# A fused attention and GeGLU block on one core: Tanh behind a row's first mark, x's transfers in front at block changes, softmax numerators divided inside the attention, output weights in the key tiles

## The chip, the core and the metric

The kernel runs on one core of a Trainium2 chip. The core has five engines with instruction streams of their own: PE (TensorE, matrix products; PEld is its loading of the stationary operand), DVE (VectorE), ACT (ScalarE), POOL (GpSimd) and SP (SyncE, which here issues all DMA transfers, in one queue). They wait for one another by semaphores. The metric is device microseconds of one execution, lower is better, given as the median of several.

## The reference

The input is x of 2048 tokens with 576 features. It is normalized (layer norm without parameters), and two things are computed from it: multi-head attention s with 32 heads of 18 features, and a gated feed-forward g with 4608 hidden values. The output is x + s * silu(g).

```python
def _A_ref(x, wqkv, wo):
    qkv = (lambda x, *d: x.transpose(*d))((x @ wqkv).reshape(B, S, 3, H, Dh), 2, 0, 3, 1, 4)
    q, k, v = qkv[0], qkv[1], qkv[2]
    scores = jnp.einsum("bhqd,bhkd->bhqk", q, k) * (Dh ** -0.5)
    p = _softmax(scores, axis=-1)
    o = jnp.einsum("bhqk,bhkd->bhqd", p, v)
    return (lambda x, *d: x.transpose(*d))(o, 0, 2, 1, 3).reshape(B, S, D) @ wo

def _B_ref(x, w_gate, w_up, w_down):
    return (_gelu(x @ w_gate) * (x @ w_up)) @ w_down

x = A_x
xn = _layernorm(x, axis=-1)
s = _A_ref(xn, A_wqkv, A_wo)
g = _silu(_B_ref(xn, B_w_gate, B_w_up, B_w_down))
return x + s * g
```

## The kernel before

**Precision.** Products are made in a 32-bit format that keeps fewer digits, so each operand is split into a high and a low part (`split` L101 on POOL, `split_av` L111 on ACT and DVE), and three products (high x high, low x high, high x low) are summed.

**Stages.** First (to about 196 us) x is normalized and transposed, q, k and v are projected and written to DRAM. Then come 144 *sections*. A section (`section` L500, products in `gate_up` L385) makes the gate and up products of 128 hidden values for one block of 512 tokens: 27 pairs of 64-row products, two of which run side by side in the upper and lower half of the array. Two sections are a *row* (256 hidden values); 18 rows make a token block, and there are 4 blocks. Sections 0 to 9 lead in; 10 to 137 (`ATT`) carry the attention; 138 to 143 carry the output projection.

**Attention.** 32 units (4 query blocks x 8 groups of 4 heads), four sections each. In a section 16 score products and 16 products for the maxima of a later unit are dealt out between the gate and up pairs. ACT turns scores into exponentials (L659), DVE reduces maxima (L624). After each odd section PE multiplies exponentials by values (L693, 64 products). Column 0 of the values is 1, so that row 0 of the result is the softmax's denominator; the numerators go to `oT` in DRAM, the denominators to `sT`, and their reciprocals (L727) to `rT`. `max_neg` and `max_end` (L626, L634) turn a unit's maxima into two more rows of its queries, by PE, ACT (`mr`) and eight transfers. Keys lie in seven buffers of two tiles each (`KS`, L564), loaded twelve transfers at a time (`load_k` L575).

**Hidden values.** `activate` (L405), behind each section: ACT squares the gate (L408); DVE makes the inner polynomial (L409); ACT copies up (L412); DVE multiplies it by the gate (L413); ACT takes Tanh (L414); DVE makes the product (L416). `finish` (L535) splits the result into hh and hl on POOL.

**Sums of a row.** In the attention a row's sums (`half_downs` L447) follow the next even section. The 8 sums (4 groups of 128 tokens x 2 column halves) are each made in two halves, of 64 rows of the contraction, six products each; halves of two sums run side by side. The second half of a sum may start only when its first is in. This is told by a *mark*: a tiny ACT instruction (L443) that waits for the last product of the first half, and for which the second half's first product waits. DVE adds each sum to Y (L427).

**x of a block.** `load_xd` (L132) loads the transposed x of the next block, six tiles, into the lower half of the partitions and copies each to the upper half on POOL (L139). There is one set of tiles: it is reloaded behind section 35, 71 and 107.

**The end.** `load_wo` (L795) loads the output weights, `load_o` (L804) a block of numerators with, row group by row group, the reciprocals broadcast over 18 rows each (`den`, L820, 13 transfers), and DVE multiplies (L822). A *place* is 128 tokens: `split_o` (L824) on POOL, `load_xy` (L830) loads x and y and makes the gate th, `project_o` (L842) makes two halves of 14 products on PE, `put` (L849) multiplies by the gate on DVE, adds x and stores. The loop at L870 does three places a section, and the last four behind the last section.

**Order.** The order of PE's instructions is that of the program (manual schedule). For all other engines a planner of the framework orders each engine's instructions by estimated times. Three means bind it: `keep_in_program_order`, `after` (L94, a wait by semaphore), and a dependency without a semaphore, which only fixes the order on one engine.

Of the kernel before, what the change touches and what calls it, by code (L numbers as in the profile page):

```python
# [8 lines left out]
F32 = mybir.dt.float32  # L9
# [8 lines left out]
P = 128  # L18
# [25 lines left out]
MROW = 3 * DH  # L44
NK = KT + 1
# [22 lines left out]
def kernel(ctx: ExitStack, tc: tile.TileContext, x, wqkv, wo, w_gate, w_up, w_down, out):  # L68
# [14 lines left out]
    rT = dram.tile([H, S], F32, name="rT")  # L83
    ys = dram.tile([S - TB, D], F32, name="ys")
# [3 lines left out]
    ident = const.tile([P, P], F32, name="ident")  # L88
    make_identity(nc, ident)
    identr = const.tile([P, P], F32R, name="identr")  # L90
    nc.gpsimd.tensor_copy(identr, ident)
# [5 lines left out]


    low_part = []
# [32 lines left out]
    def load_xd(b):  # L132

        xd = [[], []]
        for c in range(0, NC, XG):
            for i in range(2):
                t = wts.tile([P, XG, TB], F32R, name=f"xd{i}_{c}")
                nc.sync.dma_start(f(t)[0:HR], xhs[b][i, c * HR:(c + XG) * HR, :].rearrange("(k p) t -> p k t", p=HR))
                nc.gpsimd.tensor_copy(t[HR:P], t[0:HR])  # L139
                xd[i].append(t)  # L140
        return xd
# [8 lines left out]
    with tc.tile_pool(name="pro", bufs=1) as pro, tc.tile_pool(name="pps", bufs=1, space=PSUM) as pps:  # L150

# [186 lines left out]
        for b in range(NB):  # L338
# [25 lines left out]
            if b == 1:  # L364
                XD = load_xd(0)
            if b == 2:
# [11 lines left out]

    FF = {"w": ahead, "xd": XD, "down": [], "n": 0,
# [25 lines left out]
    def activate(pg, pu, early):  # L405
# [8 lines left out]
        nc.scalar.activation(t1, t1, AF.Tanh, scale=GC * GS)  # L414
        if early:
            nc.vector.scalar_tensor_tensor(t1, t1, 1.0, t2, op0=ALU.add, op1=ALU.mult)  # L416
        else:
            nc.vector.scalar_tensor_tensor(t1, t1, 1.0, pg, op0=ALU.add, op1=ALU.mult)
            nc.vector.tensor_tensor(t1, t1, pu, op=ALU.mult)
        return t1  # L420
# [26 lines left out]
    def half_downs(b, r, hs, wd, Y, middle=None):  # L447
# [52 lines left out]
    def section(specials=(), tag="f", raw_d=None, early=None):  # L500
# [8 lines left out]
        keep = tc.keep_in_program_order if n == NU * NA + len(FIRST) + 1 else lambda i: i  # L509
        nxt = load_gu((n + 1) % (NR * G), keep) if n + 1 < NF else None  # L510
        if nxt:
            for k in range(NG - 1):
                first = split_gu(nxt, k)
                if k == 0 and n in ATT and n > ATT.start:
                    tc.add_manual_dep(first.ins, FF["hl"].ins.name, mybir.DependencyInfo(
                        mybir.DependencyClass.NoSync, mybir.DependencyReason.DATA), reason="hidden values first")
# [18 lines left out]
    def finish(pool=ffn, cut=split, bufs=1):  # L535
# [5 lines left out]
        cut(hh, hl, FF["act"])  # L541
# [10 lines left out]

    todo = {}
# [8 lines left out]

    with tc.tile_pool(name="att", bufs=1, reuse_waits="tile") as att:
        KS = [[att.tile([P, TB], F32R, name=f"KS{i}{r}") for r in range(2)] for i in range(KB)]  # L564
# [4 lines left out]
        M2 = [att.tile([P, 2, HR], F32R, name=f"m2{i}") for i in range(2)]  # L569
        for mm in M2:  # L570
            nc.vector.memset(f(mm), 0.0)
# [25 lines left out]
        for i in range(TB // HR):  # L597
            nc.sync.dma_start(zq[:, i * HR:(i + 1) * HR], ident[0:HR - MROW, HR:P])

        QS, MX, ACC, SUM, PT, NM, DEN = {}, {}, {}, {}, {}, {}, {}  # L600
# [25 lines left out]
        def max_neg(u, keep=lambda i: i):  # L626
# [3 lines left out]
            m2 = NM[u] = M2[u % 2]  # L630
# [3 lines left out]
        def max_end(u, tags="mf"):  # L634

            m2 = NM.pop(u).rearrange("p i c -> p (i c)")
            pms = [ps.tile([P, TB], F32, name="pm", tag=tag, bufs=BANKS[tag])[:, 0:HR] for tag in tags]
            for a, pm in enumerate(pms):
                rr = slice(HR * a, HR * a + HR)
                nc.tensor.matmul(pm, m2[rr], identr[rr, rr], start=True, stop=True)  # L640
            mr = att.tile([P, P], F32, name="mr", bufs=1)
            for a, pm in enumerate(pms):
                nc.scalar.activation(mr[:, HR * a:HR * a + HR], pm, AF.Copy)
# [285 lines left out]
```

## Time and profile before

| what | us |
|---|---|
| median of 3 runs (2714.59 to 2718.29) | 2714.97 |
| the profiled execution | 2709.72 |
| its span, first to last instruction | 2707.9 |
| PE busy | 2573.5 |
| DVE busy | 1952.4 |
| ACT busy | 1567.7 |
| POOL busy | 1289.0 |

The span is what the profile's rows are placed in; 1.8 us of the execution lie around it. Busy times overlap, as the engines work side by side. A row of the timeline gives the start from the span's begin, the length, the engine, the line of the kernel, the operation, what is written <- read, and in brackets how long the engine stood idle and what ended that. A row of the waits gives the instruction that waited, who released it, the total, the number and the longest. PE issues a product before the last one has left the array, so a row's length is longer than its share of time; starts of neighbours give the pace.

### The profile page before, as it was taken

How to read it: one execution, taken by the hardware profiler on the slowest of the kernel's cores; microseconds unless marked ns; L12 is line 12 of the kernel's file. 1: busy time of each engine (PE TensorE's matmuls, PEld its weight loads, DVE VectorE, ACT ScalarE, POOL GpSimd, SP SyncE). 2: the span in 40 equal slices, each digit the busy share in tenths (PEclk: the TensorE clock that was granted, in tenths of full speed). 3: DMA queues.
4: the chain of work that ended last, by engine and by line, in shares of the span. 5: the costliest groups of instructions: out<-in, count | busy, mean ns of one | idle time of the engine just before them, and what ended most of it. 6: DMA issues, size and time to landing. Idle time of an engine off the chain costs nothing.

```text
span 2707.9 us, 63064 instructions
## 1 busy us (share of the span) xinstructions
PE 2573.5 (95%) x24038; PEld 2014.9 (74%) x24038; DVE 1952.4 (72%) x3470; ACT 1567.7 (58%) x3114; POOL 1289.0 (48%) x1404
## 2 busy tenths in 40 slices
PE   9999999999999999999999999999999999999578
PEld 8888777777777777777767777777777777777468
DVE  5327877788877777787877777888777777882345
ACT  3223566666656666666656666666656666666111
POOL 2127454444454444444464444444454444445354
PEclk9999999999999999999999999999999999999889
DMA  8766344344454444444464434444454444433553
GB/s 268 255 233 149 87 108 100 98 100 97 100 128 100 100 100 100 100 97 99 98 135 100 98 98 99 96 98 100 97 120 113 100 100 99 100 79 66 156 178 113
DMA packets 379564, 315.53 MB, mean 117 GB/s; under 512 B 107388, under 2 KB 289148, under 8 KB 379264
## 3 DMA queue, kind: packets, MB, share of 16 engines
q1 hardware_dynamic: 379264, 311.51, 45.6%
q8 instruction: 191, 3.13, 0.5%
q14 instruction: 109, 0.89, 0.1%
HBM read 261.38 MB, written 49.47 MB: 115 GB/s over the span
## 4 chain that ended last, share of the span: by engine, by line
PE 70%; DVE 20%; DMA 3%; issue 2%; ACT 2%; POOL 2%; SPq 1%; ACTq 0%; POOLq 0%; DVEq 0%
DVE mx L624 18%; PE pg L395 17%; PE acc L693 16%; PE py L438 14%; PE po L171 7%; PE pe L658 6%; PE pm L623 5%; PE pu L395 3%; DVE t L409 1%; PE po L846 1%; DMA den<-rT 1%; ACT t L408 1%; DMA xd<-xhs 1%; ACT pT L659 1%; DMA yy<-ys 1%
## 5 line engine op out<-in xcount | busy, mean ns | idle before, releaser
L659 ACT ACTIVATE pT<-pe 128x512 f32<-128x512 f32 x2048 | 1151.5, 598 | 389.2 <-PE pm L623 271.7
L624 DVE TENSOR_REDUCE mx<-pm 128x1 f32<-128x512 f32 x2048 | 1251.4, 682 | 168.9 <-PE pm L623 166.3
L395 PE MATMUL pu<-xd,wh 64*128 64x512 f32 x2592 | 932.6, 392 | 13.0 <-POOL xd L139 13.0
L395 PE MATMUL pg<-xd,wh 64*128 64x512 f32 x2592 | 931.5, 391 | 0.9 <-DVE thl L853 0.9
L623 PE MATMUL pm<-KS,q 64*128 64x512 f32 x2048 | 784.1, 388 | 0.0
L658 PE MATMUL pe<-q,KS 64*128 64x512 f32 x2048 | 779.3, 388 | 0.0
L395 PEld LDWEIGHTS pg<-xd,wh 64*128 64x128 f32 x2592 | 477.8, 185 | 118.2 <-POOL wh L102 49.6
L102 POOL TENSOR_SCALAR hh<-t 128x512 fp32r<-128x512 f32 x128 | 79.5, 621 | 925.4 <-DVE t L416 911.3
L395 PE MATMUL pu<-xd,wl 64*128 64x512 f32 x1296 | 503.0, 388 | 0.0
L395 PE MATMUL pg<-xd,wl 64*128 64x512 f32 x1296 | 502.7, 388 | 0.0
L395 PEld LDWEIGHTS pu<-xd,wh 64*128 64x128 f32 x2592 | 478.2, 185 | 20.3 <-POOL xd L139 15.7
L693 PE MATMUL acc<-pT,VS 128*32 128x512 f32 x4096 | 452.8, 594 | 0.0
L104 POOL TENSOR_TENSOR wl<-raw,wh 128x384 fp32r<-128x384 f32 x432 | 434.4, 1020 | 13.2
L438 PE MATMUL py<-dh,hh 64*128 64x288 f32 (+1 forms) x2160 | 351.0, 299 | 65.0 <-ACT mark L443 62.8
L623 PEld LDWEIGHTS pm<-KS,q 64*128 64x128 f32 x2048 | 375.6, 185 | 31.4 <-DVE mx L624 4.0
L658 PEld LDWEIGHTS pe<-q,KS 64*128 64x128 f32 x2048 | 371.5, 185 | 23.6
L438 PE MATMUL py<-dh,hl 64*128 64x288 f32 (+1 forms) x2160 | 344.3, 294 | 0.0
L693 PEld LDWEIGHTS acc<-pT,VS 128*32 128x32 f32 x4096 | 127.3, 110 | 289.9 <-issue 276.2
L438 PE MATMUL py<-dl,hh 64*128 64x288 f32 (+1 forms) x2160 | 342.3, 292 | 0.0
L427 DVE TENSOR_TENSOR Y<-py,Y 128x288 f32<-128x288 f32 x544 | 235.2, 455 | 136.5 <-PE py L438 136.4
L102 POOL TENSOR_SCALAR wh<-raw 128x384 fp32r<-128x384 f32 x432 | 218.1, 517 | 219.3 <-PE pu L395 156.4
L438 PEld LDWEIGHTS py<-dh,hh 64*128 64x128 f32 (+1 forms) x2160 | 219.3, 185 | 88.2 <-ACT mark L443 77.3
(121 smaller groups left out, 3115.2 us busy)
## 6 DMA issues: line engine op xcount, KB each, us to landing
KS<-qk SPq DMA_DIRECT2D x1536, 36.0 KB
raw<-in_B_w_gate_dram SPq DMA_DIRECT2D x144, 288.0 KB
raw<-in_B_w_up_dram SPq DMA_DIRECT2D x144, 288.0 KB
raw<-in_B_w_down_dram SPq DMA_DIRECT2D x67, 576.0 KB
VS<-vs SPq DMA_DIRECT2D x128, 152.0 KB
qk<-t SPq DMA_DIRECT2D x72, 256.0 KB
q<-qk SPq DMA_DIRECT2D x384, 36.0 KB
xx<-in_A_x_dram SPq DMA_DIRECT2D x32, 288.0 KB
```

The costliest lines, as they stand in the source:

```text
L102: first = nc.gpsimd.tensor_scalar(hi, raw, 1.0, 1.0, op0=ALU.mult, op1=ALU.mult)
L104: low_part[:] = [keep(nc.gpsimd.tensor_tensor(lo, raw, f(hi), op=ALU.subtract))]
L171: nc.tensor.matmul(o, st, m, start=(i == 0), stop=(i == len(terms) - 1))
L395: nc.tensor.matmul(o, w[1 + wp][k][rr, c, :], xd[xp][k][rr, c, :], start=(i == 0), stop=(i == len(terms) - 1))
L408: nc.scalar.activation(t1, pg, AF.Square)
L427: nc.vector.tensor_tensor(yy, py, yy, op=ALU.add)
L438: return nc.tensor.matmul(py, hs[g][a][rr, j * P:(j + 1) * P], wd[w][rr, g, 288 * c:288 * c + 288], start=start, stop=stop)
L623: nc.tensor.matmul(pm, QS[u, r][rr, t * P:(t + 1) * P], KS[(u * NA + c) % KB][r][rr, :], start=True, stop=True)
L624: nc.vector.tensor_reduce(MX[u][:, 2 * r + a, t, c:c + 1], pm, axis=AX.X, op=ALU.max)
L658: nc.tensor.matmul(pe, KS[(u * NA + c) % KB][r][rr, t * P:(t + 1) * P], QS[u, r][rr, :], start=True, stop=True)
L659: nc.scalar.activation(PT[u, kt][:, 2 * r + a, :], pe, AF.Exp, scale=SCALE)
L693: nc.tensor.matmul(ACC[u][32 * a:32 * a + 32, :], VS[(u * NA + c) % VB][:, v:v + 32], pt[:, a, :], start=first, stop=last, skip_group_chec ...
```

## The change

Five edits.

1. `activate` returns Tanh and what follows as a function, `rest`. Where a row's sums by halves come next, `rest` is called inside them, behind the first mark, with Tanh bound behind that mark on ACT. Elsewhere it is called at once.
2. Before the section at whose end x is exchanged, the keys are loaded first; the six transfers of x are bound behind them, the next gate and up weights behind the last of x, and the split of hh behind the last copy.
3. In the attention the numerators of units 0 to 29 are read back, in two pieces of 72 rows x 256 tokens, with their reciprocals broadcast, multiplied on POOL and stored to `oN`. Those of the last two units follow in the first section of the end, on DVE. `load_o` reads `oN`, in two transfers.
4. The output weights are loaded into the key tiles as these come free in the last six attention sections and behind them, by 16 transfers. The key tiles get a pool of their own, one tile for both halves.
5. In the end a row's sums come before the places; the places use another group of three accumulator banks; `put` adds on DVE; the two column halves are stored by one transfer, but for the last block; split numerators get three buffers instead of two, gates three instead of four.

Besides, m2 has one buffer with 48 columns a half, `mr` shares two buffers with the pieces, and the identity lives in the first stage only, with two copies of its 64x64 corner kept.

```diff
     def load_xd(b, key=None):
...
-                nc.sync.dma_start(f(t)[0:HR], xhs[b][i, c * HR:(c + XG) * HR, :].rearrange("(k p) t -> p k t", p=HR))
-                nc.gpsimd.tensor_copy(t[HR:P], t[0:HR])
+                asked[:] = [nc.sync.dma_start(f(t)[0:HR], xhs[b][i, c * HR:(c + XG) * HR, :]
+                                              .rearrange("(k p) t -> p k t", p=HR))]
+                if key:
+                    no_sync(asked[0], key, "keys first")
+                copied[:] = [nc.gpsimd.tensor_copy(t[HR:P], t[0:HR])]
...
-        nc.scalar.activation(t1, t1, AF.Tanh, scale=GC * GS)
-        if early:
-            nc.vector.scalar_tensor_tensor(t1, t1, 1.0, t2, op0=ALU.add, op1=ALU.mult)
...
+        def rest(behind=None):
+            tanh = nc.scalar.activation(t1, t1, AF.Tanh, scale=GC * GS)
+            if behind:
+                no_sync(tanh, behind, "a mark first")
+            if early:
+                nc.vector.scalar_tensor_tensor(t1, t1, 1.0, t2, op0=ALU.add, op1=ALU.mult)
...
                             elif a == 1:
                                 seen[k] = behind(one)
+                                if k == 0 and "rest" in FF:
+                                    FF.pop("rest")(seen[k])
...
+        if asked:
+            xd_last = asked.pop()
+
+            def keep(i):
+                no_sync(i, xd_last, "transposed x first")
         nxt = load_gu((n + 1) % (NR * G), keep) if n + 1 < NF else None
...
-            FF["xd"] = load_xd(b + 1)
-        FF["act"] = activate(pg, pu, n < ATT.stop)
+            FF["xd"] = load_xd(b + 1, FF["key"])
+        FF["act"], FF["rest"] = activate(pg, pu, n < ATT.stop)
+        if n not in ATT or g or not FF["down"] or not FF["down"][0][-2]:
+            FF.pop("rest")()
...
-        cut(hh, hl, FF["act"])
+        first = cut(hh, hl, FF["act"])
+        if n in ATT and copied:
+            no_sync(first, copied.pop(), "transposed x first")
...
+    def load_numbers(num, rb, g, toks):
+
+        nc.sync.dma_start(num, oT[QD * DH * g:QD * DH * (g + 1), toks])
+        nc.sync.dma_start(rb, rT[QD * g:QD * (g + 1), toks].rearrange("h (o s) -> h o s", o=1)
+                          .to_broadcast([QD, DH, toks.stop - toks.start]))
+
+    def norm_numbers(num, rb, g, toks, engine):
+        engine.tensor_tensor(num, num, rb, op=ALU.mult)
+        nc.sync.dma_start(oN[QD * DH * g:QD * DH * (g + 1), toks], num)
...
+    KT2 = [key.tile([P, 2, TB], F32R, name=f"KS{i}") for i in range(KB)]
+    KS = [[t[:, r] for r in range(2)] for t in KT2]
...
+                    for h in range(2 if u < NU - 2 else 0):
+                        at((u + 1) * NA + 3 + h, 2 * h, load_piece, u, h)
+                        at((u + 1) * NA + 4 + h, 2 * h, norm_piece, u, h)
...
+            new_x = (FF["n"] + 1) % (NR * G) == 0
+            if new_x:
+                load_k(n - 1 + KB, behind_it)
             section([p for s in range(s0, s0 + SLOTS) for p in slot_pairs(s)])
-            if n > 0:
+            if n > 0 and not new_x:
                 load_k(n - 1 + KB)
+            if n > NU * NA - KB:
+                load_wo((n - 1) % KB)
...
         def load_o(b):
...
-            nc.sync.dma_start(o[:, 0:KT, :], oT[0:R0, toks].rearrange("(k p) t -> p k t", p=P))
-            nc.sync.dma_start(o[0:HR, KT, :], oT[R0:D, toks])
-            for k in range(NK):
...
-                    nc.sync.dma_start(den[rows], rT[h:h + m, toks].rearrange("h (o s) -> h o s", o=1)
-                                      .to_broadcast([m, e - d, TB]))
-                nc.vector.tensor_tensor(o[0:n, k, :], o[0:n, k, :], den[0:n], op=ALU.mult)
+            nc.sync.dma_start(OT[b % 2][:, 0:KT, :], oN[0:R0, toks].rearrange("(k p) t -> p k t", p=P))
+            nc.sync.dma_start(OT[b % 2][0:HR, KT, :], oN[R0:D, toks])
...
             if n == NU * NA:
-                load_wo()
+                load_wo((n - 1) % KB)
...
                 load_o(0)
                 ready(2)
-            elif n < ENDS - 1:
+                for u in range(NU - 2, NU):
+                    piece = [S2[0:QD * DH, i, 0:TB] for i in range(2)]
+                    where = u % NQ, slice(S - TB, S)
+                    load_numbers(*piece, *where)
+                    norm_numbers(*piece, *where, nc.vector)
+            downs()
+            if NU * NA < n < ENDS - 1:
                 for b, j in places[done:done + 3]:
                     for c in range(2):
-                        put(b, j, c, project_o(b, j, c, "mf"[n % 2]), nc.gpsimd)
+                        put(b, j, c, project_o(b, j, c, "s"), nc.vector)
                     done += 1
                     ready(done + 2)
-            downs()
             finish(epi, cut, 2)
```

More of the change, by code (lines that the diff above doesn't have):

```diff
@@ L130, in split_gu, with load_xd @@
         return first
-    def load_xd(b):
+    def load_xd(b, key=None):
         xd = [[], []]
@@ L365 @@
                 XD = load_xd(0)
+                for i in range(TB // HR):
+                    nc.sync.dma_start(zq[:, i * HR:(i + 1) * HR], ident[0:HR - MROW, HR:P])
             if b == 2:
@@ L736, with behind_it @@
             load_q(0, (r,))
+        def behind_it(one):
+            FF["key"] = one
         slot, chunk = 0, 1
```

107 lines of the change are left out of this document (58 added, 49 removed).

## The prediction

> **What bounds the kernel now.** I read the first line of the page, then the busy time of each engine by stage, then what TensorE (PE) waited for.
>
> ```profile
> span 2707.9 us, 63064 instructions
> ```
>
> The table by stage has: stretch, length, busy time (instructions) of PE, PEld, DVE, ACT and POOL, granted clock, DMA share, GB/s. The rows are the attention from its second section on (127 sections) and the last six sections with the output projection.
>
> ```profile
> 312.97:2516.35 2203.38, 2127.60 (x21075) 1624.36 (x21073) 1698.66 (x2999) 1444.98 (x2885) 1078.44 (x1167) 1.00 0.42 100
> 2516.35:2707.90 191.55, 134.95 (x968) 123.60 (x964) 84.36 (x141) 27.09 (x45) 88.58 (x102) 0.87 0.53 155
> ```
>
> PE is the bound in the attention. It idles 2203.38 - 2127.60 = 75.8 us in the attention, and 191.55 - 134.95 = 56.6 us in the last stage, where its clock is down too (0.87). Its waits, by window (attention, then the end): total us, times, longest.
>
> ```profile
> PE py L438 <- ACT mark L443: 62.8, 63, 1.2
> PE pu L395 <- POOL xd L139: 13.0, 5, 3.8
> ```
> ```profile
> PE po L846 <- DVE thl L853: 25.9, 5, 10.3
> PE po L846 <- POOL oh L102: 21.0, 1, 21.0
> ```
>
> So three places can be won: one mark a row (63 rows), three block changes, and the end. The change has a part for each.
>
> **Part 1, Tanh behind the first mark.** One row's place, from the timeline: start, length, engine, line.
>
> ```profile
> 1427.07 0.61 ACT L412 ACTIVATE t<-pu 128x512 f32<-128x512 f32 x1
> ...
> 1427.22 0.69 DVE L409 SCALAR_TENSOR_TENSOR t<-t,pg 128x512 f32<-128x512 f32 x1 [0.29 <-ACT t L408]
> ...
> 1427.41 0.29 PE L438 MATMUL py<-dl,hh 64*128 64x288 f32 x2
> ...
> 1427.54 0.29 PE L438 MATMUL py<-dh,hl 64*128 64x288 f32 x2
> ...
> 1427.94 0.63 ACT L414 ACTIVATE t<-t 128x512 f32<-128x512 f32 x1 [0.27 <-DVE t L409]
> 1428.48 0.42 ACT L443 ACTIVATE mark<-mark 128x1 f32<-128x1 f32 x2
> 1428.61 0.69 DVE L416 SCALAR_TENSOR_TENSOR t<-t,t 128x512 f32<-128x512 f32 x1
> ...
> 1428.71 0.40 PE L438 MATMUL py<-dh,hh 64*128 64x288 f32 x2 [0.89 <-ACT mark L443]
> ...
> 1429.81 0.46 DVE L425 COPY Y<-py 128x288 f32<-128x288 f32 x1 [0.51 <-PE py L438]
> ```
>
> PE issues a pair of products each 0.13 us (1427.41 to 1427.54), so it wanted to go on at 1427.67 and did at 1428.71: 1.04 us lost. Marks 0 and 1 stand behind Tanh, and Tanh waits for the DVE product L409, which ends at 1427.91. With mark 0 in front of Tanh, it starts where the copy L412 ends, some 0.1 us early as rows on ACT do (Tanh's end 1428.57, mark's start 1428.48): 1427.58, done 0.21 later, PE at about 1427.80. Residue 0.13. The **next late thing** is mark 1: Tanh still starts at 1427.94, so mark 1 ends at 1428.69 as now, while PE wants it 6 x 0.13 after 1427.80, at 1428.58: 0.1 at most, less if PE's first pair after a stop is slow, as now (1428.71 to the next pair). I take 0.85 us a row. Behind the waiting Tanh stand the later marks on ACT, L416 on DVE and the split of hh on POOL; L416 moves by nothing, since L409 sets Tanh's start, and DVE idles 0.51 before the first sum Y. Sum: 63 x 0.85 = **53.5 us**; between 38 (0.6 a row, if mark 1 takes over more) and 65 (1.04). The score work does not swallow it: in such an even section DVE is busy 14.56 and ACT 12.63 of 17.81 us (first row of the next part).
>
> **Part 2, block changes.** The even section in front of which x is exchanged, thrice, and an ordinary one of the same kind first:
>
> ```profile
> 1305.93:1323.74 17.81, 16.63 (x186) 14.44 (x184) 14.56 (x27) 12.63 (x28) 6.83 (x10) 1.00 0.24 69
> 1374.90:1399.09 24.19, 19.04 (x186) 15.72 (x184) 15.04 (x27) 12.76 (x28) 16.17 (x18) 0.93 0.62 144
> 747.27:772.03 24.76, 19.06 (x186) 15.66 (x184) 14.95 (x27) 12.76 (x28) 16.16 (x18) 0.93 0.60 142
> 2002.10:2026.33 24.23, 20.11 (x186) 16.47 (x184) 15.04 (x27) 12.76 (x28) 16.15 (x18) 0.86 0.61 143
> ```
> ```profile
> 1381.39 1.47 POOL L139 CAST xd<-xd 64x1536 fp32r<-64x1536 f32 x1
> ...
> 1386.21 1.46 POOL L139 CAST xd<-xd 64x1536 fp32r<-64x1536 f32 x1
> ...
> 1387.72 0.50 PE L395 MATMUL pu<-xd,wh 64*128 64x512 f32 x1 [3.56 <-POOL xd L139]
> ```
>
> The three lose 6.4 + 6.9 + 6.4 = 19.7 us. The last copy (1386.21) starts 3.4 us behind the end of the copy before it, with other splits of POOL between. In the new order the six copies (8.8 us) run in front of hh. The x transfers pass the weight transfers on SP and stay behind twelve key transfers, now issued a section earlier. Moved back are hh, hl and the next weights, which are needed a section later: covered, and if that cover failed they would cost what PE waits now. PE works 7.08 us on values between the sections,
>
> ```profile
> 1409.20 7.08 PE L693 MATMUL acc<-pT,VS 128*32 128x512 f32 x64
> ```
>
> and wants the last third of x two thirds into the next. I leave 0.6 us each: **18 us**; between 10 (the transfers themselves late) and 20.
>
> After that stop the granted clock is 0.53 for the next 3.41 us:
>
> ```profile
> 1388.29:1391.70 3.41, 3.41 (x20) 2.71 (x18) 2.21 (x4) 1.79 (x3) 1.95 (x3) 0.53 0.14 13
> ```
>
> The Trainium skill, TensorE: Matmul & The Clock Gate, Part 1 (The HAM clock gate), says that an idle window of about 3.4 us halves the clock until a busy one has passed. The trace agrees here (3.56 us idle, 3.41 us slow).
>
> **Part 3, the end.** By section (the granted clock is the third number from the right):
>
> ```profile
> 2516.35:2526.07 9.72, 9.72 (x81) 8.12 (x78) 6.35 (x7) 1.23 (x2) 4.32 (x6) 1.00 0.41 114
> 2526.07:2581.96 55.89, 25.23 (x165) 22.81 (x163) 18.12 (x27) 4.48 (x7) 22.01 (x25) 0.73 0.74 211
> 2581.96:2613.94 31.98, 24.55 (x161) 22.92 (x162) 16.61 (x27) 4.86 (x7) 15.95 (x16) 0.84 0.45 134
> 2613.94:2648.99 35.05, 22.75 (x164) 20.74 (x163) 12.03 (x22) 3.00 (x5) 22.97 (x28) 0.85 0.60 184
> 2648.99:2673.06 24.07, 21.41 (x164) 19.52 (x163) 11.14 (x18) 6.45 (x9) 15.59 (x21) 1.00 0.52 154
> 2673.06:2707.90 34.84, 31.29 (x241) 29.48 (x239) 20.12 (x44) 7.07 (x15) 7.73 (x9) 1.00 0.22 66
> ```
>
> From the chain of waits, and from SP's waits:
>
> ```profile
> 2528.48 10.88 DMA den<-rT
> ...
> 2679.75 3.38 PE py L438 x24
> 2683.13 7.43 PE po L846 x56
> ```
> ```profile
> SPq L855 <- POOL thl L854: 45.2, 17, 10.2
> ```
>
> Removed: 52 denominator transfers and 20 DVE products, the first of which stood between the last attention work and the first projection (the 10.88 us); five transfers of output weights there (16 smaller ones now fall into the last six attention sections and the first behind them). Added there: six transfers and two DVE products for the last two units, needed only by the fourth block. The 24 additions go from POOL to DVE, so stores wait for DVE, where SP had stood 45.2 us on POOL with the next x, y and weights behind it; whole rows save 12 stores.
>
> What PE needs at full clock: a section is at most 2679.75 - 2673.06 = 6.7, half a row's sums 3.4, three places 6 x 14 products by 7.43/56 = 11.1; together 21.2. The first and last rows of the table stay. 9.7 + 4 x 21.2 + 34.8 = 129.3. The fourth such section already takes 24.07, 2.9 over it, with POOL's additions in it. I leave 10 us of idle time: 139.3, a gain of **52 us**; between 24 (only the start mended: 55.89 to 31.98) and 62. New first in line is the transfer of the first numerators, then POOL's splits; both lie beside section and sums.
>
> The additions' price on DVE has these rows (shortest, median, longest):
>
> ```profile
> L854 POOL TENSOR_TENSOR thl<-thl,xx x24: 787/806/1248, 2564.2 to 2672.5; 128x288 f32<-128x288 f32 x24
> ...
> L403 DVE SCALAR_TENSOR_TENSOR thl<-thl,yy x12: 752/832/2006, 2559.3 to 2658.7; 128x576 f32<-128x576 f32 x12
> ...
> L854 DVE TENSOR_TENSOR thl<-thl,xx x8: 443/448/459, 2694.8 to 2704.9; 128x288 f32<-128x288 f32 x8
> ```
>
> 24 x 0.45 = 11 us; stretched as the longest L403 is (2.4 times), 26. DVE is busy 84.36 of 191.55 and loses its 20 products, so both are covered in 139 us. The Trainium skill, GPSIMD Engine Reference, Key points, speaks against this move: GpSimd shares its SBUF interfaces with VectorE instructions that have two SBUF inputs. The 2006 ns row fits it; by it the end would be dearer by at most 15 us, were DVE the bound.
>
> **What the attention gets in return.** 30 units x 2 pieces: a 72x256 POOL product each and three transfers. No row has that product; it lies between nothing and 0.81 us (128x288, nearest), which I take: 48 us of POOL, with 1078 of 2203 busy. SP's nearest row:
>
> ```profile
> 1425.89 4.26 SPq L587 DMA_DIRECT2D KS<-qk  x11
> ```
>
> 180 x 0.39 = 70 us of SP's time over 2200. A piece is read a section (17 us) before it is used, and its numbers are a section old by then. The row transposed for the maxima shares the pieces' two buffers, but 17 us apart. I cost it at nothing, 5 us at the worst. Single m2, key tiles by pairs and the identity's new place: nothing, their users are sections apart.
>
> **Sum.** 53.5 + 18 + 52 = 123.5 us off the profiled run's 2709.72 (span 2707.9 and 1.8 around it): 2586.2. The median of the three runs is 5.25 above the profiled one, so 2591.5, say **2592**.
>
> **Rivals.**
> 1. *Mark 1 takes mark 0's place* (Tanh in front of it, or the planner puts DVE's L409 later): a row gains 0.35 instead of 0.85, 22 us: 2623. For it: both marks now stand behind one Tanh. Against: 6 products lie between their uses.
> 2. *The end stays ragged.* Transfers set it: stops over 3.4 us come back and each slows PE's next 3.41 us. The four sections then lie between 24.07 and 31.98, say at 28, and the start keeps a stop of 10: 9.7 + 10 + 4 x 28 + 34.8 = 166.5, a gain of 25 instead of 52: 2619. For it: a DMA share of 0.74 behind the attention. Against: much of that were the denominators. That is the clock rule's own way to another time.
> 3. *The change does not do it:* the planner keeps Tanh in front. Then parts 2 and 3 alone: 2592 + 53.5 = 2645.
> 4. *Slower:* a piece's product waits on POOL for its transfer, and hh, hl and the weights queue behind it. An odd section's hl is made at 1414.35 and used 12 steps before 1427.67, at 1426.1:
>
> ```profile
> 1413.07 1.28 POOL L104 TENSOR_TENSOR hl<-t,hh 128x512 fp32r<-128x512 f32 x1
> ```
>
> So each of 60 pieces must wait 12 us until anything is lost, and 12 + 123.5/60 = 14 us to eat the gain; at 15 us it is 2592 + 60 x 3 = 2772. Against it: the loads are issued a section ahead; the longest den transfer on the chain took 10.88.
>
> **How the numbers follow.** Forecast 0.72, rivals 0.10, 0.11, 0.04, 0.03. The low end is the best of all parts, 65 + 20 + 62 = 147: 2568. The high end lies above rivals 1 and 2 and near 3: 2640. What is left out is the worst of 3, and 4, and two shortfalls at once. A measurement of this kernel tells about 0.2% from no change. Faster 0.96, same 0.01, slower 0.03, all of the last in rival 4.
>
> **What would show it.** Right: waits of PE on marks below 20 us in all, mark 0 before Tanh; waits on xd below 2 us and those three sections within a us of the others; in the end no PE wait over 3.4 us and clock 1.00. Wrong: marks' waits still 40 or more (rival 1 or 3); a new PE wait on keys, hl or wh, or ACT's mr waiting on a piece (4); PE po waiting on thl or oh (2).

## The result and the profile after

| | us |
|---|---|
| before, median of 4 runs (2713.55 to 2718.29) | 2714.78 |
| after, median of 4 runs (2622.3 to 2627.97) | 2625.94 |
| ratio after/before, 95% interval | 0.9669 (0.9652 to 0.9686) |
| the profiled execution after, and its span | 2622.3, 2620.5 |

The kernel became faster by 3.3%. The prediction was 2592, with a range of 2568 to 2640: right in sign and inside the range, but 34 us too low. The span fell from 2707.9 to 2620.5, by 87.4 us, where 123.5 were predicted.

The table by stage of the changed kernel, with the columns of the prediction, first the attention from its second section on and the last stage:

```profile
313.93:2469.62 2155.69, 2149.47 (x21075) 1583.47 (x21073) 1710.80 (x2999) 1439.45 (x2885) 1120.24 (x1229) 1.00 0.45 110
2469.62:2620.50 150.88, 129.44 (x968) 119.13 (x964) 91.42 (x147) 26.87 (x45) 71.45 (x78) 0.94 0.52 153
```

The attention gained 2203.38 - 2155.69 = 47.7 us (predicted 71.5), the end 191.55 - 150.88 = 40.7 (predicted 52). PE idles 6.2 us in the attention, where it idled 75.8. But it is *busy* for 2149.47 us where it was busy for 2127.60, with the same number of instructions (21075): 22 us of the gain were given back where nobody waits.

PE's waits of the changed kernel over the whole span (total us, times, longest):

```profile
PE py L457 <- DVE Y L446: 12.8, 3, 5.9
PE py L457 <- DVE dl L116: 3.3, 1, 3.3
PE py L457 <- ACT mark L462: 2.5, 5, 0.9
PE po L897 <- DVE Y L446: 1.5, 1, 1.5
```

The waits on marks are gone (62.8 us in 63 rows before), those on x's tiles (`xd`, 13.0) too. What is left in the end is mostly a wait on the sums Y: 12.8 + 1.5 us, where PE waited 2.0 us on them before.

**A row's place**, from the timeline of the same row as in the prediction:

```profile
1401.16 0.61 ACT L426 ACTIVATE t<-pu 128x512 f32<-128x512 f32 x1
...
1401.64 0.21 ACT L462 ACTIVATE mark<-mark 128x1 f32<-128x1 f32 x1
1401.64 0.29 PE L457 MATMUL py<-dh,hl 64*128 64x288 f32 x2
...
1401.90 0.40 PE L457 MATMUL py<-dh,hh 64*128 64x288 f32 x2
...
1402.03 0.63 ACT L430 ACTIVATE t<-t 128x512 f32<-128x512 f32 x1 [0.18 <-DVE t L423]
1402.14 0.30 PE L457 MATMUL py<-dl,hh 64*128 64x288 f32 x2
```

Read it with the prediction's: the mark starts 0.13 us ahead of the end of the copy's row, Tanh (L430) comes behind it, and PE goes on 0.26 us after its last pair, where it needs 0.13. What is left is that 0.13 and a slow first pair (1401.90 to 1402.14).

**The block changes.** The three sections with new x, and the ordinary one of the same kind last:

```profile
742.50:759.95 17.45, 17.02 (x186) 14.58 (x184) 14.91 (x27) 12.54 (x28) 13.59 (x16) 1.00 0.90 182
1354.95:1372.86 17.91, 17.04 (x186) 14.61 (x184) 15.35 (x27) 12.53 (x28) 13.01 (x16) 1.00 0.84 175
1968.02:1985.19 17.17, 17.01 (x186) 14.57 (x184) 14.64 (x27) 12.54 (x28) 12.53 (x14) 1.00 0.88 180
```
```profile
1286.96:1304.13 17.17, 17.04 (x186) 14.61 (x184) 14.63 (x28) 12.53 (x28) 6.03 (x9) 1.00 0.31 81
```

They lose 0.3 + 0.7 + 0.0 = 1.0 us, where they lost 19.7.

**The end by section:**

```profile
2469.62:2479.39 9.77, 9.77 (x81) 8.58 (x78) 6.34 (x7) 1.23 (x2) 3.92 (x6) 1.00 0.42 125
2479.39:2509.50 30.11, 22.68 (x164) 20.66 (x163) 13.92 (x25) 3.69 (x6) 12.78 (x15) 0.89 0.77 241
2509.50:2541.19 31.69, 23.89 (x164) 21.81 (x163) 19.24 (x25) 5.43 (x8) 23.74 (x26) 0.84 0.72 189
2541.19:2564.72 23.53, 21.09 (x164) 19.34 (x163) 14.57 (x24) 3.69 (x6) 13.86 (x16) 1.00 0.52 163
2564.72:2585.54 20.82, 20.82 (x164) 19.30 (x163) 16.39 (x25) 5.87 (x8) 11.55 (x11) 1.00 0.32 99
2585.54:2620.50 34.96, 31.20 (x241) 29.45 (x239) 20.94 (x44) 6.95 (x15) 5.59 (x6) 1.00 0.25 75
```

The fourth full section runs without a stop: 20.82 us is what PE needs (21.2 predicted). The first two take 30.11 and 31.69, and their clock is at 0.89 and 0.84. So two questions stand: what made the attention's work itself slower, and what stops the end.

**What stops the end**, from DVE's timeline there (in brackets the idle time before, and what ended it):

```profile
2480.07 0.45 DVE L446 TENSOR_TENSOR Y<-py,Y 128x288 f32<-128x288 f32 x1
2487.74 2.33 DVE L417 SCALAR_TENSOR_TENSOR thl<-thl,yy 128x576 f32<-128x576 f32 x2 [7.22 <-ACT thl L416]
...
2492.78 0.76 DVE L417 SCALAR_TENSOR_TENSOR thl<-thl,yy 128x576 f32<-128x576 f32 x1 [1.50 <-ACT thl L416]
2493.45 0.68 DVE L423 SCALAR_TENSOR_TENSOR t<-t,pg 128x512 f32<-128x512 f32 x1
2494.05 0.81 DVE L446 TENSOR_TENSOR Y<-py,Y 128x288 f32<-128x288 f32 x2
...
2500.44 0.69 DVE L589 TENSOR_TENSOR S<-S 72x512 f32<-72x512 f32 x1 [4.55 <-DMA S<-oT]
```

DVE takes its instructions in a fixed order. Here a gate (L417) comes before the next sums, and its Tanh on ACT waits for yy. DVE stands 7.22 us, and the additions Y (L446), which set PE's banks free, stand behind it; at 2500.44 it stands again, before the numerators of the last unit. yy was asked for in time, but behind the o of two blocks. SP's timeline:

```profile
2474.82 0.39 SPq L873 DMA_DIRECT2D OT<-oN  x1
...
2475.87 0.54 SPq L873 DMA_DIRECT2D OT<-oN  x1
...
2477.68 0.44 SPq L890 DMA_DIRECT2D yy<-ys  x1
```

The first Tanh of a gate starts 9.4 us behind that issue:

```profile
2487.03 0.69 ACT L416 ACTIVATE thl<-yy 128x576 f32<-128x576 f32 x1 [8.63 <-DMA yy<-ys]
```

### The profile page after: what moved, and what is told of

It reads as the page before. It is cut to its first block, busy times and chain, and to the rows that moved or that the text cites. A ratio compares the mean times of both kernels' runs of the same rounds, so it can differ in the third digit from the quotient of the medians.

```text
span 2620.5 us, 63379 instructions
## 1 busy us (share of the span) xinstructions
PE 2590.0 (99%) x24038; PEld 1970.0 (75%) x24038; DVE 1972.1 (75%) x3475; ACT 1561.9 (60%) x3114; POOL 1313.5 (50%) x1442
## 3 DMA queue, kind: packets, MB, share of 16 engines
q1 hardware_dynamic: 390712, 320.95, 47.8%
## 4 chain that ended last, share of the span: by engine, by line
PE 83%; DVE 13%; DMA 2%; issue 1%; ACT 1%; SPq 0%; ACTq 0%; DVEq 0%
PE pg L409 20%; PE acc L749 17%; PE py L457 15%; DVE mx L680 10%; PE pe L714 8%; PE pu L409 8%; PE po L181 7%; PE pm L679 6%; PE po L897 2%; DMA yy<-ys 1%; DVE t L423 1%; ACT pT L715 0%; PE pt L242 0%; DVE nm L685 0%; DVE m L687 0%
## 5 line engine op out<-in xcount | busy, mean ns | idle before, releaser
L680 DVE TENSOR_REDUCE mx<-pm 128x1 f32<-128x512 f32 x2048 | 1266.6, 683 | 148.3 <-PE pm L679 145.6
L679 PE MATMUL pm<-KS,q 64*128 64x512 f32 x2048 | 793.2, 393 | 0.0
L714 PE MATMUL pe<-q,KS 64*128 64x512 f32 x2048 | 787.4, 392 | 0.0
L457 PE MATMUL py<-dh,hh 64*128 64x288 f32 (+1 forms) x2160 | 356.5, 305 | 19.2 <-DVE Y L446 12.8
L446 DVE TENSOR_TENSOR Y<-py,Y 128x288 f32<-128x288 f32 x544 | 234.6, 454 | 85.7 <-PE py L457 81.8
L409 PEld LDWEIGHTS pg<-xd,wl 64*128 64x128 f32 x1296 | 239.5, 185 | 34.2
```

The lines of the kernel that those rows point to most:

```text
L409: nc.tensor.matmul(o, w[1 + wp][k][rr, c, :], xd[xp][k][rr, c, :], start=(i == 0), stop=(i == len(terms) - 1))
L446: nc.vector.tensor_tensor(yy, py, yy, op=ALU.add)
L457: return nc.tensor.matmul(py, hs[g][a][rr, j * P:(j + 1) * P], wd[w][rr, g, 288 * c:288 * c + 288], start=start, stop=stop)
L679: nc.tensor.matmul(pm, QS[u, r][rr, t * P:(t + 1) * P], KS[(u * NA + c) % KB][r][rr, :], start=True, stop=True)
L680: nc.vector.tensor_reduce(MX[u][:, 2 * r + a, t, c:c + 1], pm, axis=AX.X, op=ALU.max)
L714: nc.tensor.matmul(pe, KS[(u * NA + c) % KB][r][rr, t * P:(t + 1) * P], QS[u, r][rr, :], start=True, stop=True)
```

## The experiments

Each kernel was run on the chip beside the kernel before (2712 to 2714 us in these runs). Unless a number of rounds is named, a time is of one run. Sections are compared by the start of their first product in each trace; a table gives the medians.

### Which part gives what, and what slowed the attention

The changed kernel's attention is slow from its first sections on, ahead of any piece and of any row whose Tanh moved (section 10 takes 13.87 us instead of 13.72, section 11 20.53 instead of 20.37). So one candidate was the place of a tile in the on-chip memory: the change shrinks m2 (two buffers of 512 bytes to one of 384), and the queries behind it move by 128 bytes modulo 256.

**Part 1 alone**, in the kernel before: `rest` behind the first mark, nothing else.

```diff
+        def rest(behind=None):
+            tanh = nc.scalar.activation(t1, t1, AF.Tanh, scale=GC * GS)
+            if behind:
+                no_sync(tanh, behind, "a mark first")
...
+                                if k == 0 and "rest" in FF:
+                                    FF.pop("rest")(seen[k])
```

> The kernel before with part 1 alone (Tanh behind a row's first mark). Theory P (the slower pace of the changed kernel's sections, 0.16 us each in odd sections that no mark touches, comes from where the tiles lie): even sections 0.80 us shorter than before (17.39 to 16.6), odd ones unchanged at 16.88, marks' waits of PE under 5 us, span about 2707.9 - 63 x 0.80 = 2657. Rival T (the new order on ACT sets another rhythm between PE's two halves): odd sections 17.05 as in the changed kernel, even ones 0.64 shorter, span about 2707.9 - 63 x 0.64 + 65 x 0.16 = 2678.

Measured 2664.62, span 2662.8.

**The identity's new place alone**, and **the narrow m2 alone**, in the kernel before:

```diff
-    ident = const.tile([P, P], F32, name="ident")
...
+        ident = pro.tile([P, P], F32, name="ident")
```
```diff
-        M2 = [att.tile([P, 2, HR], F32R, name=f"m2{i}") for i in range(2)]
+        M2 = att.tile([P, 2, MH], F32R, name="m2")
```

> The kernel before with the identity moved into the first stage's pool alone, which puts every later tile 768 bytes (3 x 256) lower and leaves their distances. Theory P in the form that the queries' place against keys and x counts, to 256 bytes: pace unchanged, odd sections 16.88, even 17.39, span within 2 us of 2707.9 but for the first stage. Rival I (the place itself counts): odd sections 17.05, even 17.55, span about 20 us longer.

> The kernel before with the one narrow m2 alone (one buffer of 2 x 48 instead of two of 2 x 64): the queries and all behind them lie 640 bytes (2.5 x 256) lower, keys, x and weights stay. Theory P (queries against keys and x to 256 bytes: 160 and 160 before, 32 and 160 in the changed kernel and here): odd sections 17.05, even 17.55, span about 128 x 0.16 = 20 us longer, 2728. Rivals T and I: pace unchanged, 2708.

Measured 2714.13 for the first: nothing. Measured 2731.46 for the second: *slower* by 19 us than the kernel before beside it (2712.38), though it only makes a buffer smaller.

**The changed kernel with two small tiles, of 128 bytes together, put ahead of the queries** (they are allocated behind them otherwise); no instruction changes.

```diff
         nc.vector.memset(f(M2), 0.0)
+        att.tile([P, QD * TB // P], F32, name="sums", bufs=2)
```

> The changed kernel with 128 bytes put in front of the queries (the small tile for the denominators is laid there), so that they lie at 160 of 256 bytes as keys and x do. Theory P: odd sections back at 16.88, even ones at 16.6, span 2620.5 - 128 x 0.16 = 2600. Rivals T and I: pace as in the changed kernel, 17.05 and 16.75, span 2620.

Measured 2602.51, against 2626 for the changed kernel. The attention, in this kernel:

```profile
313.18:2449.70 2136.52, 2129.37 (x21075) 1600.65 (x21073) 1694.08 (x2999) 1436.67 (x2885) 1119.77 (x1229) 1.00 0.45 111
```

That is 19.2 us less (2155.69 to 2136.52), and PE's busy time fell by as much and a little more (2149.47 to 2129.37). But the exponentials pT had moved along with the queries in every kernel so far.

**The same 128 bytes behind the queries instead**: pT moves, the queries do not.

```diff
             load_q(0, (r,))
+        att.tile([P, QD * TB // P], F32, name="sums", bufs=2)
```

> The changed kernel with the two small sums tiles between the queries and the pT tiles: the queries stay at 32 bytes modulo 256 as in the changed kernel, the pT tiles (the probabilities, which the sums over keys and the values read) go to 160 as in the kernel before. Nothing is left out. Theory P, narrow form (it is the queries' place): the attention stays slow, even rows 16.75 and 17.17, odd 17.04, time 2622 to 2626. The rival within P (it is pT's place, which moved along in every run so far): even rows 16.59 and 17.0, odd 16.88, time 2600 to 2606.

Measured 2626.52: as slow as the changed kernel. The addresses here come from the compiled programs; the keys, which are read beside the queries, start at 160 bytes modulo 256 in all of them. Even sections are of two kinds, without and with the turning of the maxima.

| kernel | queries mod 256 | pT mod 256 | odd section | even sections (two kinds) |
|---|---|---|---|---|
| before | 160 | 160 | 16.89 | 17.39, 17.81 |
| e2, identity moved | 160 | 160 | 16.88 | 17.39, 17.81 |
| e3, narrow m2 | 32 | 32 | 17.05 | 17.55, 17.96 |
| e1, Tanh alone | 160 | 160 | 16.88 | 16.59, 17.00 |
| after | 32 | 32 | 17.04 | 16.75, 17.17 |
| e4, 128 bytes ahead of the queries | 160 | 160 | 16.88 | 16.59, 17.02 |
| e10, 128 bytes behind the queries | 32 | 160 | 17.05 | 16.75, 17.17 |

The column of the queries sorts the sections without an exception. One odd section each of after and of e4, in which PE never idles (busy time = length):

```profile
1269.91:1286.96 17.05, 17.05 (x156) 10.84 (x154) 12.98 (x23) 10.65 (x19) 10.40 (x11) 1.00 0.62 136
```
```profile
1260.80:1277.69 16.89, 16.89 (x156) 10.44 (x154) 12.84 (x23) 10.63 (x19) 10.36 (x11) 1.00 0.62 133
```

And in it PE's timeline, the first product of the first and of the last of 14 pairs that follow one another, first after, then e4. Six of the 14 pairs hold a product with queries streamed (pe) and one with queries loaded (pm); the other eight are gate and up products, which read no queries:

```profile
1271.76 0.39 PE L714 MATMUL pe<-q,KS 64*128 64x512 f32 x1
...
1274.77 0.39 PE L679 MATMUL pm<-KS,q 64*128 64x512 f32 x1
```
```profile
1262.66 0.39 PE L715 MATMUL pe<-q,KS 64*128 64x512 f32 x1
...
1265.61 0.39 PE L680 MATMUL pm<-KS,q 64*128 64x512 f32 x1
```

13 steps take 3.01 and 2.95 us: 0.2315 and 0.2269 a pair, in the mean of both sorts. The records' own lengths (0.39) show nothing; only the starts do. Over the whole attention the mean step (steps over 0.4 us left out) from a pair with queries to the next of gate and up is 0.2329 in after and 0.2274 in e4, from gate and up to one with queries 0.2339 and 0.2306, and between two of gate and up 0.2295 and 0.2275. So most of the loss lies beside the pairs with queries.

From e1's rows part 1 is worth 17.39 - 16.59 = 0.80 and 17.81 - 17.00 = 0.81 us a row, so 50 us over 63 rows. The whole run gained a little less: 2712.38 - 2664.62 = 47.8.

**The changed kernel with Tanh at once**, from the other side:

```diff
-        if n not in ATT or g or not FF["down"] or not FF["down"][0][-2]:
-            FF.pop("rest")()
+        FF.pop("rest")()
```

> The changed kernel with part 1 undone: Tanh is issued at once, in front of the row's first mark. If a row's gain of 0.80 us is part 1 alone: even sections 17.55 instead of 16.75 (17.97 where the maxima are turned), marks' waits of PE back at 60 us or more, odd sections unchanged at 17.05, span 2620.5 + 63 x 0.80 = 2671. Rival (the other parts carry some of it): less than 0.4 a row, span below 2646.

Measured 2669.48, span 2667.7: 47.2 us more than the span of after, and the wait is back whole:

```profile
PE py L457 <- ACT mark L462: 63.1, 63, 1.2
```

### What stops the end

Three single causes first, each on the changed kernel: the last unit's two products of numerators moved from DVE to POOL; a fourth buffer for the gates (the low parts of o give one up); the next block's o asked for two places later.

```diff
-                    norm_numbers(*piece, *where, nc.vector)
+                    norm_numbers(*piece, *where, nc.gpsimd)
```
```diff
-            th = epi.tile([P, D], F32, name="thl", bufs=3)
+            th = epi.tile([P, D], F32, name="thl", bufs=4)
```
```diff
-                if j == 0 and b + 1 < NB:
+                if j == 2 and b + 1 < NB:
                     load_o(b + 1)
```

> The changed kernel with the two products of the last units on POOL instead of DVE. Theory Q (in the end PE waits for sums that DVE cannot add since DVE stands, in its fixed order, before an instruction whose transfer is not there: the first gate, the second of these products, later gates): the section with 30.1 us loses about the 4.5 us that DVE stood before the second product, 26, and the end 150.7 becomes about 146. Rival Y (the y transfers alone set the pace): 150 as now, the wait moves to the next gate.

> The changed kernel with four gates' buffers as before the change (and two low parts of the numerators instead of three, to make room). Theory B (the third buffer's loss made ACT's gate Tanh wait for a store to land, 45.9 us over eight places, and the section's square stands behind it on ACT): ACT's waits on the store below 10 us, the section with 31.7 us at 27, the end at about 146. Rival Y (y's transfers set it): waits of ACT move from the store to y, the end within 2 us of 150.7.

> The changed kernel with the second block's numerators (1.2 MB) asked for two places later, and so on for each block. Theory Q with transfers as the cause of the first stop: the first y, issued behind both blocks' numerators, lands at 9.3 us after its issue now and 4 to 5 earlier here; PE's first stop of 5.9 us falls to about 2 and its clock stays up: the section with 30.1 us at 24 to 26. Rival: later blocks' numerators come too late for their splits, and the next sections lose what the first gains (end 150 or more).

Measured 2618.81, 2622.19 and 2624.23; the end takes 148.5, 150.8 and 151.5 us (150.7 after, counted alike). POOL gave 2.2, half of what was expected; the others gave nothing. Even the 2.2 is not clear of chance: the end of e10, which only moves tiles, took 153.8. With four gate buffers PE's waits on Y are 17.6 us in all, more than before the edit. But ACT still waits 39.7 us on stores before its gates, where it waited 45.9 and below 10 was expected, so this edit did not take the waits on stores away and does not rule them out. With the later o PE's longest wait on Y is 9.2 us, where 5.9 was to fall to 2. So none of these three edits alone mends the end.

**The order itself**, on e4: the gates of the row blocks are bound behind the section's sums on DVE and behind its own Tanh on ACT; the loads stay where they were.

```diff
+            if late:
+                no_sync(tanh, FF["tanh"], "the section first")
+                no_sync(g, FF["sum"], "the sums first")
...
                 for b, j in places[done:done + 3]:
+                    late_gate(b, j)
```

> The base is the changed kernel with the queries back at 160 bytes modulo 256 (2602.51, end 150.8). Here the gates of the row-blocks below the last block come, on DVE and on ACT, only behind the section's sums and behind its own Tanh; xx and yy are loaded as early as before. Nothing is left out of the computation. Theory Q (DVE stands in its fixed order at a gate whose yy has not landed, with the sums that free PE's banks behind it): the stop of 5.9 us at the second end section and the next two go, the sections of 30.1, 30.3 and 25.1 come down to 21 to 25, the end to 135 to 143, the time to 2587 to 2595. Theory T (the transfers and thl's buffers themselves hold the end; whatever stands in front only shows it): the wait moves behind the sums, to the products with po, and the end stays within 3 us of 150.8, the time within 3 of 2602.5.

Measured 2601.59, the end 149.2: 7 us above the bounds of theory Q (the engines' fixed order is what stops the end), and within those of theory T (the transfers and buffers themselves). PE now waits longest for the projection's products, 7.6 us on DVE's gating of an earlier place, as T said, and 3.5 us on a sum. DVE does not stand at the first gates any more:

```profile
2471.22 0.69 DVE L592 TENSOR_TENSOR S<-S 72x512 f32<-72x512 f32 x1 [8.93 <-DMA S<-oT]
2471.83 0.68 DVE L426 SCALAR_TENSOR_TENSOR t<-t,pg 128x512 f32<-128x512 f32 x1
2472.43 0.45 DVE L449 TENSOR_TENSOR Y<-py,Y 128x288 f32<-128x288 f32 x1
```

Now the last unit's numerators stand before their transfer with a sum behind. The third full section went from 25.09 in e4 to 20.82, which is all that PE needs.

**All that stood there out of the way**, on e9: a third buffer for yy, and the two products of numerators a section or two later on POOL (5 rounds).

```diff
-                yy = epi.tile([P, D], F32, name="yy", bufs=2)
+                yy = epi.tile([P, D], F32, name="yy", bufs=3)
...
+            if n in (NU * NA + 1, NU * NA + 2):
+                piece = [S2[0:QD * DH, i, 0:TB] for i in range(2)]
+                where = (n - NU * NA + NU - 3) % NQ, slice(S - TB, S)
+                load_numbers(*piece, *where)
+                norm_numbers(*piece, *where, nc.gpsimd)
```

> e9's order of the gates on the same base (2601.6, end 149.2), and the other instructions that stood before transfers there taken out of the way: yy in three buffers, so that the third row-block's yy of a section is asked for with the others (the low parts of o in two instead, to make room), and the last unit's two products of numerators, which stood 8.9 and 4.7 us on DVE before S<-oT with a sum behind, moved to the next two sections and to POOL. Nothing is left out. Theory Q (the stops are engines standing in their fixed order before transfers that were asked for too late): the sections of 33.0 and 30.1 come to 21 to 25, like the two that are at 20.8 already, the end to 128 to 136, the time to 2580 to 2588. Theory T (traffic: DMA is 73% busy in these sections, and each wait removed shows the next): the end stays above 143, the time above 2595.

Measured 2594.96 (2594.58 to 2595.2), ratio to before 0.9565 (0.9552 to 0.9578); the end 142.9. That is just below the bounds of theory T (143, and 2595) and 7 us above those of Q. The first two full sections of the end, and PE's longest wait there:

```profile
2459.75:2494.78 35.03, 24.06 (x164) 22.06 (x163) 13.21 (x24) 5.38 (x8) 21.65 (x25) 0.81 0.76 210
2494.78:2516.54 21.76, 21.09 (x164) 19.54 (x163) 15.29 (x24) 3.59 (x6) 14.00 (x14) 1.00 1.01 294
```
```profile
PE po L907 <- POOL ol L107: 9.6, 2, 8.9
```

The second section is all but clean; the first waits for a cut of o on POOL, which itself stood 4.4 us before the transfer of up weights with that cut behind it.

**That moved too**: the second block's o asked for behind the third yy, three buffers for the low parts of o again, the numerators behind the first five cuts of o (5 rounds).

```diff
-                if j == 0 and b + 1 < NB:
+                if j == 3 and b + 1 < NB:
                     load_o(b + 1)
...
+                    no_sync(norm_numbers(*piece, *where, nc.gpsimd), OO["last"], "o first")
```

> e11 (2594.96, end 142.9, of which the section behind the attention 35.0) with what stood before a transfer there moved again: the second block's o is asked for behind the third row-block's yy, the low parts of o have their third buffer back (the third yy lies in S2 instead), and the two products of numerators stand on POOL behind the cuts of the first five row-blocks' o, in the idle tiles of the down weights. Nothing is left out. Theory Q: the wait of 8.9 us for ol's cut on POOL (POOL stood 4.4 us before raw<-w_up with it behind) and that of 2.0 on the third gate go, the section comes from 35.0 to 23 to 28, the end to 128 to 136, the time to 2580 to 2588. Theory T (traffic: the two sections move 212 and 271 GB/s): what is asked for later lands later, the end stays above 140, the time above 2592.

Measured 2593.63 (2591.55 to 2596.35), ratio 0.9557 (0.9543 to 0.957); the end 143.8. Within the two intervals this is the same time as e11's, and both numbers are as theory T said. The sections swapped; their rows, and then one row of DVE's timeline in the second:

```profile
2460.24:2481.09 20.85, 20.85 (x164) 19.28 (x163) 13.10 (x23) 5.28 (x8) 14.01 (x15) 1.00 0.75 213
2481.09:2517.96 36.87, 23.86 (x164) 22.11 (x163) 18.16 (x25) 3.58 (x6) 26.00 (x27) 0.77 0.89 245
```
```profile
2496.38 0.47 DVE L919 TENSOR_TENSOR thl<-thl,xx 128x288 f32<-128x288 f32 x1 [16.34 <-DMA xx<-in_A_x_dram]
```

The first runs at PE's own pace, as theory Q said; in the second DVE stands 16.34 us before xx, with the cut of the down weights behind it, and PE waits for that:

```profile
PE py L460 <- DVE dl L116: 13.0, 1, 13.0
```
```profile
2487.11 0.33 SPq L891 DMA_DIRECT2D xx<-in_A_x_dram  x1
```

The wait has moved once more, and the sum stays. A late issue and a slow transfer are both in this stand: SP asked for xx only when DVE had stood 7.1 of the 16.34 us, and the transfer then took 9.2, while the DMA engines were busy for 0.94 of the stand.

A part of why the sum stays can be read from the DMA share. Length times share, over the first two full sections:

| kernel | length of both | DMA busy in them |
|---|---|---|
| after | 61.8 | 30.11 x 0.77 + 31.69 x 0.72 = 46.0 |
| e11 | 56.8 | 35.03 x 0.76 + 21.76 x 1.01 = 48.6 |
| e12 | 57.7 | 20.85 x 0.75 + 36.87 x 0.89 = 48.4 |

PE needs 2 x 20.82 = 41.6 for both. What is transferred there keeps the DMA engines busy for 46 to 48.6 us, so at such rates 4 to 7 us of stop are left whatever the order, unless traffic leaves these sections. This is an estimate from these rows, and not a lower bound. By bytes, after moves 30.11 x 241 + 31.69 x 189 GB/s = 13.2 MB in them. That takes 45 us at the 294 GB/s of e11's second section, but 39 us at the rate of the fastest 20 us of the first stage of after, which has other transfers:

```profile
164.00:184.00 20.00, 20.00 (x94) 16.46 (x93) 4.15 (x6) 3.59 (x6) 8.40 (x8) 1.00 0.95 337
```

Of the 61.8 - 41.6 = 20.2 us that are lost in after, some 4 to 7 are of this kind by that estimate (theory T). The rest would be standing in order (theory Q) and the slow clock behind each stop; the runs do not separate them further. Of the 20.2 the order's experiments (e11, e12) won 5 and 4 us in these two sections, and in the third section all of its 2.7. That an order wins more was not shown.

e11 and e12 beat both kernels: 2594 to 2595 us against 2626 and 2715. The larger part of what they win over the changed kernel is the queries' place (2602.51 in e4).

## Why the prediction was right and where it failed

**Part 1: right.** 0.85 us a row were predicted and 0.80 came (e1): 50 us by the sections, 47 to 48 by whole runs (e1, e5), instead of 53.5. The steps held: the mark starts with the copy's end, 1401.64; Tanh still starts with the end of DVE's product; PE resumes 0.13 late. The second mark, which rival 1 had as the new late thing, cost next to nothing: PE's waits on all marks are 2.5 us. Rivals 1 and 3 fell.

**Part 2: right.** 18 predicted, 19.7 - 1.0 = 18.7 came. The last copy runs in front of the split of hh, as the POOL rows show:

```profile
1358.91 1.47 POOL L145 CAST xd<-xd 64x1536 fp32r<-64x1536 f32 x1 [0.95 <-PE pg L409]
1360.48 0.62 POOL L105 TENSOR_SCALAR hh<-t 128x512 fp32r<-128x512 f32 x1
```

**"Single m2, key tiles by pairs and the identity's new place: nothing, their users are sections apart": failed.** That argument looks for waits, and there is none. The narrow m2 moved the queries by 128 bytes modulo 256, and the steps between PE's pairs became longer: 19.2 us of the attention (e4), 0.15 to 0.16 a section. e3 shows it without the rest of the change, e10 that it is the queries and not pT. This term, put at nothing, is the largest error of the sum. The Trainium skill, SBUF — State Buffer, SBUF: two separate sides, states that PE has ports of its own and never waits there. That sentence is about engines waiting for one another, and what is measured here lies beside it: the place of an operand changed PE's mean step by 2% (0.2269 to 0.2315), in a way that shows in no wait.

**Part 3: the mechanism right, a size wrong.** Of the terms 9.7 + 4 x 21.2 + 34.8 the trace has 9.77, 20.82 (where nothing stops) and 34.96. The term "I leave 10 us of idle time" was mis-sized: 150.88 - (9.77 + 4 x 20.82 + 34.96) = 22.9. The sign that the prediction had named for it, no PE wait over 3.4 us and a clock of 1.00, did not come: PE stopped for 5.9 us in the first full section and 4.5 in the second. The reason given for it, that the new first transfers "lie beside section and sums", overlooked DVE's and ACT's fixed order: a gate before its yy holds the sums behind it. And the traffic was set aside as mostly the denominators'. By the prediction's own rows the first two full sections held 55.89 x 0.74 + 31.98 x 0.45 = 55.8 us of DMA time before; without the denominators they hold 46.0, and they were to be run in 2 x 21.2 = 42.4.

The price of the additions was not the bound, but the sharing with POOL, which the prediction named, is seen. The gates' product on DVE, shortest, median, longest:

```profile
L417 DVE SCALAR_TENSOR_TENSOR thl<-thl,yy x12: 757/1342/2133, 2487.7 to 2570.6; 128x576 f32<-128x576 f32 x12
```

The median was 832 before. Laid beside POOL's rows, the three with next to no POOL instruction beside them took 757 or 758 ns, and the four that lie wholly beside a cut of o on POOL (`ol<-OT,oh`, then `oh<-ol`) 2116 to 2133.

**The rivals.** Rival 2 (2619) came near the time by other terms: it gave the end 25 us of gain, and the end gained 40.7. Its mechanism is half there: stops above 3.4 us came back with slow clock (0.89, 0.84), for two of the four sections, though on the sums Y and not on thl or oh, which it had named as its sign. Rival 4 named a wait that did come: POOL's products of pieces waited 232.3 us in all for their reciprocals, 48 times, 9.1 at the longest. That is below the 12 us from which PE would have paid, and PE paid nothing. The products themselves took 731 ns in the mean, near the 0.81 us that was taken for them.

**The sum.** 123.5 were predicted and 87.4 came. Of the 36 missing, 19 are the queries' place in the attention, 11 the end, and 1 the first stage (the second attention section starts at 313.93 instead of 312.97). The 5 left are about what part 1 fell short of its 53.5, by the 47 to 50 us above, less the 0.7 that part 2 gave more. With the queries' place mended and the end's order partly mended, e12 stands at 2593.6.

## What to carry to other kernels

Compare not only what an engine waits for but how long it is busy with the same instructions: a change that only shrinks a buffer can shift what lies behind it, and the loss is found by the spacing of neighbouring products, not by any wait. Where a stage is short of transfers, look for the engine that stands in its fixed order before one of them, and at what stands behind it; but take the DMA share times the length first: at the same rates an order cannot win below that.

## What the runs showed of the hardware

In a stream of pairs of 64-row products that run side by side in the array, gate and up pairs with pairs of keys and queries between them, PE's mean step from pair to pair is 0.2269 us with queries and keys both at 160 bytes modulo 256, and 0.2315 with the queries at 32. Only these two places were seen. Whether the place itself counts or its distance to the keys and the other operands, what other places do, and the cause, stay open.

DVE's gate product (128x576, two inputs from the on-chip memory) took 0.757 us with no POOL instruction beside it, and 2.12 to 2.13 with a cut of o on POOL beside it all the time.
